# One Trainium2 kernel, one core: a list scheduler that knows the shared SBUF port, weight remainders on VectorE only, and float16 conversions on ScalarE or GpSimd

## The chip, the core and the metric

The kernel runs on one core of a Trainium2 chip. TensorE (PE in the profile; PEld is its weight load) multiplies, VectorE (DVE), ScalarE (ACT) and GpSimd (POOL) do the element-wise work, SyncE (SP) issues every DMA. The metric is device time in microseconds, the median of several executions. All times here are microseconds unless a row says ns.

## The reference, cut to what matters

```python
def _attn_ref(q, k, v, proj):                       # (2, 8, 768, 64), proj (64, 6)
    q_bucket = sum(((q @ proj) > 0) * powers)       # 6 hash bits
    k_bucket = sum(((k @ proj) > 0) * powers)
    scores = where(q_bucket == k_bucket, (q @ k.T) / 8, -1e9)
    attn = exp(scores - max(scores)); attn /= sum(attn) + 1e-9
    return attn @ v

def _moe_ref(x, domain_probs, w1, w2):              # x (1536, 512), 4 experts, F = 1024
    p = domain_probs / (domain_probs.sum(-1) + 1e-9)
    return sum(p[:, e:e+1] * (relu(x @ w1[e]) @ w2[e]) for e in range(4))

def _moe2_ref(x, w_in, w_out, g_ln):                # 512 -> 1024 -> 512
    h = x @ w_in
    solu = h * softmax(h)
    ln = (solu - mean(solu)) / sqrt(var(solu) + 1e-6) * g_ln
    return ln @ w_out
```

The three are chained: attention gives x, the experts take it, the second layer follows.

## The kernel before, in words

The 1536 tokens are four chunks of three tiles of 128. For each chunk come attention (8 heads), 32 expert steps, and the second layer. Precision is kept by splitting each factor into a high part and a remainder (the rounded value, and what rounding lost), so a product is three matmuls: high by high, high by remainder, remainder by high.

An expert step (`moe_a`, `moe_b`) is 12 matmuls of 384 columns (`PS<-xh,wsa` and `PS<-xl,wsa`) and 9 of 512 (`PS<-wsb,hh` and `PS<-wsb,hx`). Between them ScalarE writes the high part of the hidden values (`hh<-PS`) and VectorE their remainder (`hx<-PS,hh`). Weights come in two streams (`Stream`): a block of 128x1024 is loaded (`wra`, `wrb`), ScalarE rounds it (`wsa<-wra`, `wsb<-wrb`), and a subtraction makes the remainder (`wsa<-wra,wsa`, `wsb<-wrb,wsb`). That subtraction runs on GpSimd for all 64 first-layer expert blocks and for the 16 second-layer blocks of the first chunk, on VectorE for the rest.

Attention of the first chunk comes first and alone (`attn_first`). That of each later chunk is spread over the expert steps of the chunk before it (`attn_steps`, `Fill`). A row of 128 queries goes through scores (`PS<-kC,qC`, `PS<-kB,qB`), row maximum on VectorE (`sm<-PS`), two one-column instructions, the exponential on ScalarE (`p<-PS,sm`), a float16 high part on ScalarE (`h<-p,sm`) and its remainder on VectorE (`l<-p,sm,h`). The scores' PSUM buffer exists once (`s_b`, cap 1), so the next row's scores wait for this row's exponential. Two transposing DMAs bring a row's float16 parts into a buffer `t16`; after three rows, two conversions of 128x2304 elements to the type of the matmul (`t<-t`, line 886) follow, and `PS<-t,vs` multiplies with v. Conversions run on GpSimd (`pcopy`). The float64 weights of the second layer are decoded during the first chunk's experts (`decode_steps`: `ln<-ln`, later `y<-y`).

The order of all this is not written by hand. `Recorder` takes the instructions in program order, finds which needs which, and `emit` lays them out by a list schedule: it holds a clock and, for each engine, a heap of instructions that are ready; a free engine takes the one with the lowest place in program order (`turn_at`, less an advance given by `ahead`). How long an instruction takes in this plan is the estimate of `cost`; how long the next one must wait behind it is in `HOPS` and `OWN`. On the chip the engines then run their lists in that order, each waiting for what it needs.

Of the kernel before, what the change touches and what calls it, by code (L numbers as in the profile page):

```python
# [23 lines left out]
class Line:  # L24
    """PSUM buffers that get their places in program order."""
# [4 lines left out]
class Bank:  # L30
    """A kind of PSUM buffer: n banks in a row from one of `starts`, at most `cap` of it in use at once."""
# [10 lines left out]
class Slot:  # L42
    """A PSUM buffer whose place is chosen when the instructions are put in order."""
# [9 lines left out]
class View:  # L53
    """A part of a Slot, seen as an access pattern."""
# [28 lines left out]
class Recorder:  # L83
    """Takes the instructions in program order and emits them in an order in which the
    engines wait little: a list schedule over the dependences between the regions they touch."""

    READS = ("in_", "in0", "in1", "lhsT", "rhs", "identity", "scalar", "scalar1", "scalar2", "scale", "bias")
    # from the end of an instruction to the start of one that needs it, by their engines
    HOPS = dict(AG=0.17, AT=0.16, AV=0.1, GT=0.13, GV=0.1, TA=0.2, TG=0.22, TV=0.2, VA=0.2, VG=0.18, VT=0.2)
    OWN = dict(A=0.05, G=0.1, V=0.1, T=0.0)  # L90
# [10 lines left out]
    def engine(self, name):  # L101
        rec = self

        class Engine:
            def __getattr__(self, method):
                return lambda **kw: rec.add(name, method, kw)

        return Engine()

    @contextmanager  # L110
    def ahead(self, n):
        """Instructions that go before others of up to n places earlier."""
        self.boost += n
        yield
        self.boost -= n

    @contextmanager
    def group(self):
        """Instructions of one engine that stay together."""
        self.open = dict(eng=None, calls=[], cost=0.0, reads=[], writes=[], slots=[])  # L120
        yield
        op, self.open = self.open, None
        if op["calls"]:
            self.commit(op)
# [52 lines left out]
    def cost(self, name, method, kw, reads):  # L177
        out = kw["out"] if "out" in kw else None
        n = 1
        for d in list(out.ap)[1:]:  # L180
            n *= d[1]
        ptr = 0.06 * sum(1 for key in ("scalar", "scalar1", "scalar2") if not isinstance(kw.get(key, 0.0), (int, float, type(None))))
        if name == "T":
            if method == "transpose":
                return 0.057 if kw["in_"].dtype == F32R else 0.108
            return n * (4 if kw["rhs"].dtype == F32 else 1) / 2400 + 0.003
        if name == "A":
            ptr = 0.093 * sum(1 for key in ("scale", "bias") if not isinstance(kw.get(key, 0.0), (int, float)))
            psum = str(kw["in_"].space).endswith("PSUM")
            return (0.05 if psum else 0.092) + n / 1200 + ptr + (0.09 if "accum_out" in kw else 0)  # L190
        if name == "V":
            if method == "tensor_reduce":
                n = 1
                for d in list(kw["in_"].ap)[1:]:
                    n *= d[1]
                return 0.065 + n / 960
            fast = method in ("tensor_scalar", "tensor_copy") and not str((kw.get("in0") or kw.get("in_")).space).endswith("PSUM")
            return 0.065 + n / (1920 if fast else 960) + ptr
        if name == "G":
            return 0.095 + n * (2.16 if method == "tensor_tensor" else 0.9) / 1000  # L200
        size = SIZE[out.dtype]
        for d in list(out.ap)[:1]:
            n *= d[1]
        return n * size / 360e3

    def add(self, name, method, kw):
        def aps(keys):
# [4 lines left out]

        fn = getattr(self.engines[name], method)
        reads = [self.region(x) for x in aps(self.READS)]
        writes = [self.region(x) for x in aps(("out", "accum_out"))]
        cost = self.cost(name, method, kw, reads)
        if method == "memset":
            kw = dict(ap=kw["out"], constant=kw["value"])
        op = dict(
            eng=name,  # L220
            calls=[(fn, kw)],
            cost=cost,
            reads=reads,
            writes=writes,
            turn=method == "dma_start_transpose",
# [6 lines left out]
        assert g["eng"] in (None, name)  # L232
        g["eng"] = name
        g["turn"] = False
        g["calls"] += op["calls"]
        g["cost"] += op["cost"]
# [27 lines left out]
    def emit(self):  # L264
# [12 lines left out]
        wire = 0.0  # L277
# [14 lines left out]

        for i in range(n):
            if not left[i]:
                heappush(events, (0.0, i, None))
        order = []
        now = 0.0
        while len(order) < n:
            while events and events[0][0] <= now + 1e-9:
                _, i, slot = heappop(events)  # L300
                if slot is not None:
# [3 lines left out]
                    for j in blocked:  # L305
                        heappush(ready[ops[j]["eng"]], (ops[j]["turn_at"], j))
                    blocked.clear()
                elif i >= 0:
                    heappush(ready[ops[i]["eng"]], (ops[i]["turn_at"], i))
            for e in ready:  # L310
                if free[e] > now + 1e-9:
                    continue
                while ready[e]:
                    i = heappop(ready[e])[1]
                    if all(x.base is not None or place(x) for x in ops[i]["slots"]):
                        break
                    blocked.append(i)
                else:
                    continue
                if any(x.kind.line for x in ops[i]["slots"]):  # L320
                    for j in blocked:
                        heappush(ready[ops[j]["eng"]], (ops[j]["turn_at"], j))
                    blocked.clear()
                o = ops[i]
                order.append(i)
                if e == "S":
                    free[e] = now + (1.18 if o["turn"] else 0.48)
                    wire = max(wire, now + 1.2) + (0.67 if o["turn"] else o["cost"])
                    done = wire + 0.95
# [7 lines left out]
                for j in users[i]:  # L337
                    to = ops[j]["eng"]
                    hop = 0.0 if e == "S" else self.OWN[e] if to == e else self.HOPS.get(e + to, 0.1)
# [12 lines left out]
def lsh_attention_moe_solu(  # L352
# [28 lines left out]
    # rows of hash bits: 8 for a bit's product with its complement on the other side, 8 for the reverse  # L381
# [3 lines left out]
    # the order of the weight streams holds for these  # L385
# [11 lines left out]
    # token tiles: tile r of batch b holds the tokens 6 p + r  # L397
# [16 lines left out]
    class Ring:  # L414
        """Buffers that are used in turn."""
# [57 lines left out]

    def sub(eng, out, a, b):
        eng.tensor_tensor(out=out, in0=a, in1=b, op=ALU.subtract)

# [15 lines left out]
    def consts_a():  # L492
        """What the projections need: column h*128 + 8j + h, and 64 on its low part, of lhs_w is projection j for head h."""
# [22 lines left out]
    # rows of kD: low parts, high parts, bits; of qD: high, low, high, bits  # L516
# [6 lines left out]
    def proj_steps(c, is_k, nat, tb, pp, stks, br=None, hls=hl_r, heads=range(H)):  # L523
        """Split k or q into parts, transpose them, write stacks and hash bits."""
# [63 lines left out]
        # every product of rows is 0 for equal bits and -C for unequal ones, so a match adds exact zeros only  # L588
# [49 lines left out]
    def row_max(ps, E):  # L638
# [5 lines left out]
        # a row without a match has the same weight everywhere  # L644
# [58 lines left out]
    def row(U, rr, sb, E, pr_=p_r):  # L703
        """Probabilities of 128 queries, not yet divided by their sum."""
# [7 lines left out]
    def attn_first():  # L712
        """Projections and attention of the first chunk: nothing else runs yet."""
# [22 lines left out]
        # stacks of all heads stay where the first weights will go  # L736
# [24 lines left out]
        # the heads from FH on use float32 products: they cost the tensor engine more and the others less  # L761
# [25 lines left out]
        # two buffers for probabilities: tiles of keys 0-3 and 4-5, high and low parts  # L787
# [70 lines left out]
    def attn_steps(c):  # L858
# [8 lines left out]
        for h in range(H):  # L867
# [17 lines left out]
            for a in range(2):  # L885
                pcopy(t32[:, a, :, 0:N], d16[:, a, :, 0:N])
# [10 lines left out]
    def decode_steps(units, n, buf):  # L897
        """float64 to float32, n columns at a time: (source, factor per row or None, destination)."""
# [6 lines left out]
        for i, (src, g, dst) in enumerate(units):  # L905
# [4 lines left out]
            # exponent field to float32's, cut off at zero and infinity  # L910
# [3 lines left out]
            # mantissa in [1, 2], its 52 bits rounded to float32's  # L914
# [25 lines left out]
    def decode_a():  # L940
        """w_in and the first rows of w_out."""
# [12 lines left out]
    class Stream:  # L954
        """Weights in the order of use: [128, 4, 256] or [128, 2, 512], split into parts."""
# [10 lines left out]
        def load(self, i):  # L966
            while self.nl <= min(i, len(self.items) - 1):
                t = wr_r[self.kind].next()
                SP.dma_start(out=t, in_=self.items[self.nl][0])
# [3 lines left out]
        def split(self, i):  # L973
            while self.ns <= min(i, len(self.items) - 1):
# [4 lines left out]
                sub(self.items[self.ns][1], w[1], t, f(w[0]))  # L979
# [10 lines left out]
    def add_moe1(c, lo, hi):  # L990
        for m in range(lo, hi):
            e, fp = divmod(m, NF // 2)
            i1["m", c, m] = len(W1.items)
            W1.items.append((w1[e][:, fp * 256:fp * 256 + 256].rearrange("(k p) f -> p k f", p=128), G))
# [420 lines left out]
```

## Time and profile before

| | us |
|---|---|
| median of 3 timed runs | 1026.81 (1024.26 to 1030.49) |
| span of the profiled execution | 1014.7 |
| PE busy | 922.6 (91%) |
| DVE busy | 719.9 (71%) |
| ACT busy | 533.6 (53%) |
| POOL busy | 427.9 (42%) |

The page of the profiled execution gives as its own time the span from its first to its last instruction, 1014.7 us; the median of the timed runs is 12.1 us above it. Busy is time in which an engine executes, its waits for a port inside an instruction included.

### The profile page before, as it was taken

To read this page: it belongs to the slowest core of one execution; us is meant where nothing else is said; L and a number is where in the kernel's file an instruction comes from. 1 tells how busy PE (TensorE), PEld (TensorE's weight loads), DVE (VectorE), ACT (ScalarE), POOL (GpSimd) and SP (SyncE) were. 2 spreads that over 40 slices of the span, in tenths; PEclk is the share of its full clock that TensorE was granted. 3 is DMA by queue.
4 is the path that set the end of the run, shared out by engine and by line. 5 is a ranking of instruction groups with operands and counts; after the bars stand their busy time and mean duration, and the time that the engine had idled before them with its cause. 6 is when DMAs were issued, how large, how long until landed. Compare 5 with 4: busy or idle time off the path is not lost. (4 is left out here: it accounts for less than half of the span.)

```text
span 1014.7 us, 14292 instructions
## 1 busy us (share of the span) xinstructions
PE 922.6 (91%) x4864; PEld 818.1 (81%) x4864; DVE 719.9 (71%) x1242; ACT 533.6 (53%) x855; POOL 427.9 (42%) x333
## 2 busy tenths in 40 slices
PE   6789799787879998999999999999999999999997
PEld 5576688676768887887788898798889897999986
DVE  5765567999898888778877569868874556343564
ACT  4667346554544565665556457655553464333433
POOL 5568446575575152246444414344644031122100
PEclk9899899999998999999999999999999999999999
DMA  7166788998877786799879668868863333433400
GB/s 186 40 194 203 233 226 187 244 224 199 225 200 194 243 282 213 187 235 224 188 172 264 187 167 184 227 180 206 207 167 116 123 104 125 155 126 125 157 31 31
DMA packets 216809, 182.20 MB, mean 180 GB/s; under 512 B 127520, under 2 KB 183712, under 8 KB 216736
## 3 DMA queue, kind: packets, MB, share of 16 engines
q1 hardware_dynamic: 216736, 181.29, 66.5%
q8 instruction: 38, 0.62, 0.2%
q14 instruction: 35, 0.29, 0.1%
HBM read 127.89 MB, written 22.09 MB: 148 GB/s over the span
## 5 line engine op out<-in xcount | busy, mean ns | idle before, releaser
L348 PE MATMUL PS<-xh,wsa 128*128 128x384 f32 x1024 | 289.3, 344 | 16.2 <-DVE hx L348 8.1
L348 PE MATMUL PS<-wsb,hh 128*128 128x512 f32 x928 | 295.3, 400 | 0.5 <-DVE y L348 0.5
L348 POOL TENSOR_TENSOR wsa<-wra,wsa 128x1024 fp32r<-128x1024 f32 x64 | 160.1, 2502 | 286.9 <-ACT wsa L348 281.5
L348 PEld LDWEIGHTS PS<-xh,wsa 128*128 128x128 f32 x1024 | 192.1, 193 | 24.3 <-DVE hx L348 9.6
L348 PEld LDWEIGHTS PS<-wsb,hh 128*128 128x128 f32 x928 | 172.7, 191 | 25.9 <-DVE y L348 1.0
L348 PE MATMUL PS<-wsb,hx 128*128 128x512 f32 x464 | 185.0, 399 | 0.8 <-DVE hx L348 0.8
L348 PE MATMUL PS<-xl,wsa 128*128 128x384 f32 x512 | 174.8, 342 | 0.0
L348 POOL TENSOR_SCALAR t<-t 128x2304 fp32r<-128x2304 f16 x48 | 119.4, 2498 | 87.2 <-DMA t<-h 74.9
L348 ACT ACTIVATE p<-PS,sm 128x768 f32<-128x768 f32 x96 | 95.1, 991 | 103.2 <-DVE sm L348 86.3
L348 ACT ACTIVATE hh<-PS 128x384 fp32r<-128x384 f32 (+2 forms) x162 | 77.8, 485 | 119.5 <-PE PS L348 118.8
L348 DVE TENSOR_TENSOR wsb<-wrb,wsb 128x1024 fp32r<-128x1024 f32 x62 | 97.4, 1572 | 38.1 <-ACT wsb L348 37.7
L348 DVE SCALAR_TENSOR_TENSOR l<-p,sm,h 128x768 f16<-128x768 f32 x72 | 107.1, 1488 | 16.9 <-ACT h L348 16.7
L348 DVE SCALAR_TENSOR_TENSOR hx<-PS,hh 128x384 fp32r<-128x384 f32 x128 | 70.2, 549 | 63.9 <-ACT hh L348 63.2
L348 DVE TENSOR_REDUCE sm<-PS 128x1 f32<-128x768 f32 x96 | 91.0, 951 | 20.5 <-PE PS L348 19.8
L348 PEld LDWEIGHTS PS<-wsb,hx 128*128 128x128 f32 x464 | 88.5, 191 | 21.0 <-DVE hx L348 1.5
L348 ACT ACTIVATE wsb<-wrb 128x1024 fp32r<-128x1024 f32 x78 | 82.5, 1057 | 40.4 <-PE PS L348 30.3
L348 PEld LDWEIGHTS PS<-xl,wsa 128*128 128x128 f32 x512 | 98.9, 193 | 4.3
L348 ACT ACTIVATE wsa<-wra 128x1024 fp32r<-128x1024 f32 x78 | 82.1, 1053 | 14.5 <-PE PS L348 8.6
L348 ACT ACTIVATE h<-p,sm 128x768 f16<-128x768 f32 x72 | 67.2, 933 | 35.5 <-issue 21.9
L348 PE MATMUL PS<-kC,qC 128*128 128x384 f32 x144 | 52.4, 364 | 21.6 <-ACT p L348 21.3
L348 PE MATMUL PS<-kB,qB 80*128 80x384 f32 x192 | 67.1, 349 | 4.8 <-DMA qB<-qD 4.8
L348 PE MATMUL PS<-t,vs 128*128 128x384 f32 x312 | 61.7, 343 | 4.9 <-ACT stk L348 1.4
(169 smaller groups left out, 1330.5 us busy)
## 6 DMA issues: line engine op xcount, KB each, us to landing
wra<-in_moe_w_dram SPq DMA_DIRECT2D x64, 512.0 KB, 4.0
wrb<-in_moe_w_dram SPq DMA_DIRECT2D x64, 512.0 KB, 4.4
kC<-kD SPq DMA_DIRECT2D x24, 384.0 KB, 3.9
wra<-winD SPq DMA_DIRECT2D x16, 512.0 KB, 3.7
wrb<-woutD SPq DMA_DIRECT2D x16, 512.0 KB, 4.3
kB<-kD SPq DMA_DIRECT2D x24, 240.0 KB, 4.4
vr<-in_v_dram SPq DMA_DIRECT2D x28, 192.0 KB, 3.8
qD<-stk SPq DMA_DIRECT2D x27, 192.0 KB, 4.0
```

Source lines behind the costliest of these rows:

```text
L348: fn(**{key: x.at(x.slot.base) if isinstance(x, View) else x for key, x in kw.items()})
```

## The change: what it does

Four things are edited (the comments are also taken out).

1. The plan's estimates: each matmul costs 12.5 ns over its columns, where it was 3 ns; hops, DMA times and small instructions get new values.
2. The plan has a lock named `port`. GpSimd's instructions other than memsets, VectorE's with two SBUF inputs, and VectorE's copies and scalar operations from SBUF hold it; none of them is started in the plan while another holds it.
3. All remainders of weights are subtracted on VectorE.
4. An instruction may have forms on several engines. The two conversions of a head have one on ScalarE and one on GpSimd; the plan gives them to the engine that is free first. It has put 26 of the 48 on ScalarE, 22 on GpSimd.

```diff
-    HOPS = dict(AG=0.17, AT=0.16, AV=0.1, GT=0.13, GV=0.1, TA=0.2, TG=0.22, TV=0.2, VA=0.2, VG=0.18, VT=0.2)
-    OWN = dict(A=0.05, G=0.1, V=0.1, T=0.0)
+    HOPS = dict(AG=0.2, AT=0.17, AV=0.15, GA=0.2, GT=0.18, GV=0.13, TA=0.22, TG=0.22, TV=0.22, VA=0.13, VG=0.18, VT=0.18)
+    OWN = dict(A=0.05, G=0.22, V=0.11, T=0.0)
...
-            return n * (4 if kw["rhs"].dtype == F32 else 1) / 2400 + 0.003
+            return (n * 4 / 2400 + 0.004 if kw["rhs"].dtype == F32 else n / 2400 + 0.0125), False
...
+            two = n > 2 and sum(not psum(x) for x in ins) == 2
+            fast = n > 2 and method in ("tensor_scalar", "tensor_copy") and not psum(ins[0])
+            ptr = 0.06 * (tensor("scalar") + tensor("scalar1") + tensor("scalar2"))
+            return 0.066 + n / (1920 if fast else 960) + ptr + (0.07 if "accum_out" in kw else 0), two or fast
         if name == "G":
-            return 0.095 + n * (2.16 if method == "tensor_tensor" else 0.9) / 1000
+            if method == "tensor_tensor":
+                return 0.04 + n * 2.27 / 1000, True
+            return (0.19 if n <= 2 else 0.045 + n * 0.93 / 1000), method != "memset"
...
+                    if o["forms"][e]["port"] and port > now + 1e-9:
+                        later.append(i)
...
+                    if form["port"]:
+                        port = done
...
+    def copy_by(names, out, in_):
+
+        forms = dict(
+            G=("tensor_scalar", dict(out=out, in0=in_, scalar1=1.0, scalar2=1.0, op0=ALU.mult, op1=ALU.mult)),
+            A=("activation", dict(out=out, in_=in_, func=ACTF.Copy)),
+            V=("tensor_copy", dict(out=out, in_=in_)),
+        )
+        rec.add([(name, *forms[name]) for name in names])
...
-                pcopy(t32[:, a, :, 0:N], d16[:, a, :, 0:N])
+                copy_by("AG", t32[:, a, :, 0:N], d16[:, a, :, 0:N])
...
-                sub(self.items[self.ns][1], w[1], t, f(w[0]))
+                sub(V, w[1], t, f(w[0]))
```

The order moves on every engine. On POOL, in the first chunk's expert steps while the second chunk's attention runs beside them, this stood before (`ln` is the decoding, `t_86` the converted probabilities, `vs` the high part of v):

```order
L348 TENSOR_SCALAR ln_113<-ln_113 128x512
L348 TENSOR_TENSOR wsa_106<-wra_102,wsa_106 128x1024
L348 TENSOR_TENSOR wsb_109<-wrb_105,wsb_109 128x1024
L348 TENSOR_TENSOR wsa_107<-wra_103,wsa_107 128x1024
L348 TENSOR_TENSOR wsb_108<-wrb_104,wsb_108 128x1024
L348 TENSOR_SCALAR t_86<-t_84 128x2304 x2
L348 TENSOR_TENSOR wsa_106<-wra_102,wsa_106 128x1024
L348 TENSOR_TENSOR wsb_109<-wrb_105,wsb_109 128x1024
L348 TENSOR_SCALAR vs_74<-vr_73 128x6x64
L348 TENSOR_SCALAR ln_113<-ln_113 128x512
```

At the same place POOL now has:

```order
L387 TENSOR_SCALAR ln_113<-ln_113 128x512
L387 TENSOR_SCALAR t_86<-t_84 128x2304
L387 TENSOR_SCALAR vs_74<-vr_73 128x6x64
L387 TENSOR_SCALAR ln_113<-ln_113 128x512
L387 TENSOR_SCALAR t_86<-t_85 128x2304
L387 TENSOR_SCALAR ln_113<-ln_113 128x512
```

The subtractions have left, and of each pair of conversions one is left. On DVE, a little earlier in the same steps, the row maxima and the decoding stood like this before:

```order
L348 SCALAR_TENSOR_TENSOR hx<-PS,hh 128x384
L348 TENSOR_SCALAR ln_113<-ln_113 128x512 x3
L348 SCALAR_TENSOR_TENSOR ln_113<-ln_113 128x512 x2
L348 TENSOR_TENSOR ln_113<-ln_113 128x512
L348 SCALAR_TENSOR_TENSOR hx<-PS,hh 128x384
L348 TENSOR_REDUCE sm_87<-PS 128x1
L348 TENSOR_SCALAR sm_87<-sm_87 128x1 x3
```

Now the subtractions of both weight streams stand between them:

```order
L387 TENSOR_TENSOR wsa_107<-wra_103,wsa_107 128x1024
L387 TENSOR_TENSOR wsb_108<-wrb_104,wsb_108 128x1024
L387 SCALAR_TENSOR_TENSOR hx<-PS,hh 128x384
L387 TENSOR_SCALAR ln_113<-ln_113 128x512 x3
L387 SCALAR_TENSOR_TENSOR ln_113<-ln_113 128x512 x2
L387 SCALAR_TENSOR_TENSOR hx<-PS,hh 128x384
L387 TENSOR_TENSOR ln_113<-ln_113 128x512
L387 TENSOR_TENSOR wsa_106<-wra_102,wsa_106 128x1024
L387 TENSOR_TENSOR wsb_109<-wrb_105,wsb_109 128x1024
L387 SCALAR_TENSOR_TENSOR hx<-PS,hh 128x384
L387 TENSOR_REDUCE sm_87<-PS 128x1
```

So VectorE has two more instructions of 1024 elements in front of a row maximum. On ACT, in the same steps, a conversion now stands between a row's high part and the next row's exponential:

```order
L387 ACTIVATE hh<-PS 128x384
L387 ACTIVATE p_79,sm_88<-PS,sm_88 128x768
L387 ACTIVATE h_81<-p_79,sm_88 128x768
L387 ACTIVATE t_86<-t_84 128x2304
L387 ACTIVATE p_77,sm_89<-PS,sm_89 128x768
L387 ACTIVATE ln_113<-ln_113 128x512
L387 ACTIVATE hh<-PS 128x384
```

Before, no instruction on ACT was of this size: the conversion was POOL's.

## Rows read from the trace of the kernel before

**Rows 1.** The page: span, and busy time of each engine.

```profile
span 1014.7 us, 14292 instructions
...
PE 922.6 (91%) x4864; PEld 818.1 (81%) x4864; DVE 719.9 (71%) x1242; ACT 533.6 (53%) x855; POOL 427.9 (42%) x333
```

**Rows 2.** Windows: busy time by engine in six stages; PEclk is the granted clock.

```profile
0.00:108.00 108.00, 86.92 (x452) 70.12 (x452) 67.68 (x134) 65.40 (x130) 65.42 (x139) 0.94 0.56 163
108.00:340.00 232.00, 195.45 (x951) 172.41 (x950) 194.91 (x292) 116.01 (x182) 134.02 (x74) 0.95 0.83 212
340.00:424.00 84.00, 75.85 (x445) 67.82 (x445) 73.01 (x154) 50.74 (x88) 28.47 (x27) 0.96 0.77 237
424.00:662.00 238.00, 224.56 (x1197) 201.17 (x1196) 185.05 (x330) 140.27 (x221) 103.78 (x54) 0.99 0.85 205
662.00:968.00 306.00, 299.88 (x1572) 271.31 (x1571) 172.24 (x259) 144.92 (x211) 96.23 (x41) 1.00 0.51 148
968.00:1014.70 46.70, 39.90 (x258) 35.25 (x256) 27.00 (x79) 16.29 (x26) 0.00 (x0) 1.00 0.08 29
```

**Rows 3.** Windows: a stretch of the last chunk's expert steps, same columns.

```profile
862.00:962.00 100.00, 100.00 (x504) 90.52 (x503) 42.50 (x49) 38.57 (x52) 23.95 (x10) 1.00 0.41 136
```

**Rows 4.** Waits of PE from 108 to 340 us: in total, times, longest.

```profile
PE PS L348 <- ACT p L348: 12.4, 11, 3.0
```

**Rows 5.** Groups by form, DVE, 108 to 340 us: busy, mean ns.

```profile
L348 DVE SCALAR_TENSOR_TENSOR l<-p,sm,h 128x768 f16<-128x768 f32 x24 | 37.9, 1579 | 5.6 <-ACT h L348 5.6
L348 DVE TENSOR_SCALAR ln<-ln 128x512 int32<-128x512 int32 x36 | 32.9, 950 | 3.3 <-DMA ln<-in_moe_w_in_dram 3.2
...
L348 DVE SCALAR_TENSOR_TENSOR ln<-ln 128x512 int32<-128x512 int32 x12 | 12.6, 1049 | 0.6 <-POOL ln L348 0.5
L348 DVE SCALAR_TENSOR_TENSOR ln<-ln 128x512 f32<-128x512 uint32 x12 | 12.5, 1038 | 0.4 <-ACT ln L348 0.4
...
L348 DVE TENSOR_TENSOR ln<-ln 128x512 f32<-128x512 f32 x8 | 11.3, 1410 | 0.1
L348 DVE TENSOR_TENSOR hl<-vr,hl 128x384 fp32r<-128x384 f32 x7 | 9.4, 1342 | 0.0
L348 DVE TENSOR_TENSOR vs<-vr,vs 128x384 fp32r<-128x384 f32 x8 | 8.6, 1070 | 0.3 <-POOL vs L348 0.3
```

**Rows 6.** Timeline of DVE, five stretches: start, duration of single or merged instructions.

```profile
139.11 0.69 DVE L348 TENSOR_TENSOR ln<-ln 128x512 f32<-128x512 f32 x1
...
243.12 0.55 DVE L348 TENSOR_TENSOR vs<-vr,vs 128x384 fp32r<-128x384 f32 x1
...
245.21 1.08 DVE L348 TENSOR_SCALAR ln<-ln 128x512 int32<-128x512 int32 x3
...
398.88 1.22 DVE L348 TENSOR_TENSOR wsb<-wrb,wsb 128x1024 fp32r<-128x1024 f32 x1
...
405.12 1.01 DVE L348 SCALAR_TENSOR_TENSOR l<-p,sm,h 128x768 f16<-128x768 f32 x1
```

**Rows 7.** Timeline of DVE and POOL around 249 us.

```profile
248.60 2.90 DVE L348 SCALAR_TENSOR_TENSOR ln<-ln 128x512 int32<-128x512 int32 x1
...
248.55 2.41 POOL L348 TENSOR_TENSOR wsa<-wra,wsa 128x1024 fp32r<-128x1024 f32 x1 [1.55 <-ACT wsa L348]
```

**Rows 8.** Groups by form, POOL, 108 to 340 us.

```profile
L348 POOL TENSOR_TENSOR wsb<-wrb,wsb 128x1024 fp32r<-128x1024 f32 x15 | 39.9, 2661 | 6.0 <-ACT wsb L348 6.0
L348 POOL TENSOR_SCALAR t<-t 128x2304 fp32r<-128x2304 f16 x16 | 37.4, 2348 | 12.3 <-DMA t<-h 6.9 <-DMA t<-l 5.2
L348 POOL TENSOR_TENSOR wsa<-wra,wsa 128x1024 fp32r<-128x1024 f32 x15 | 37.4, 2491 | 45.2 <-ACT wsa L348 43.8 <-DMA kB<-kD 1.4
```

**Rows 9.** Groups by form, whole span: POOL's moved work, ACT's nearest copy.

```profile
L348 POOL TENSOR_TENSOR wsa<-wra,wsa 128x1024 fp32r<-128x1024 f32 x64 | 160.1, 2502 | 286.9 <-ACT wsa L348 281.5 <-PE PS L348 3.9 <-DMA kB<-kD 1.4
L348 POOL TENSOR_SCALAR t<-t 128x2304 fp32r<-128x2304 f16 x48 | 119.4, 2498 | 87.2 <-DMA t<-h 74.9 <-DMA t<-l 7.1 <-issue 3.7
...
L348 ACT ACTIVATE wsb<-wrb 128x1024 fp32r<-128x1024 f32 x78 | 82.5, 1057 | 40.4 <-PE PS L348 30.3 <-issue 4.4 <-DMA wrb<-woutD 2.7
```

More of the change, by code (lines that the diff above doesn't have):

```diff
@@ L118, in group @@
     def group(self):
-        self.open = dict(eng=None, calls=[], cost=0.0, reads=[], writes=[], slots=[])
+        self.open = dict(forms={}, turn=False, reads=[], writes=[], slots=[])
         yield
         op, self.open = self.open, None
-        if op["calls"]:
+        if op["forms"]:
             self.commit(op)
@@ L175, in covers, with cost, size @@
         return x[0] <= y[0] and y[1] <= x[1] and all(any(a <= c and d <= b for a, b in x[2]) for c, d in y[2])
[L177 to L182, printed above, removed]
+    @staticmethod
+    def cost(name, method, kw):
+        tensor = lambda key: kw.get(key) is not None and not isinstance(kw[key], (int, float))
+        psum = lambda ap: str(ap.space).endswith("PSUM")
+        def size(ap):
+            n = 1
+            for d in list(ap.ap)[1:]:
+                n *= d[1]
+            return n
+        n = size(kw["out"])
@@ L197, in cost @@
-            fast = method in ("tensor_scalar", "tensor_copy") and not str((kw.get("in0") or kw.get("in_")).space).endswith("PSUM")
-            return 0.065 + n / (1920 if fast else 960) + ptr
-        if name == "G":
-            return 0.095 + n * (2.16 if method == "tensor_tensor" else 0.9) / 1000
-        size = SIZE[out.dtype]
+                return 0.063 + size(kw["in_"]) / 960, False
+            if method in ("reciprocal", "memset"):
+                return 0.07 + n / 960, False
+            ins = [kw[key] for key in ("in_", "in0", "in1") if tensor(key)]
@@ L202, in cost, with add, aps @@
+        out = kw["out"]
+        parts = 128
+        for ap in (out, kw["in_"]):
+            if str(ap.space).endswith("SBUF"):
+                parts = list(ap.ap)[0][1]
         for d in list(out.ap)[:1]:
             n *= d[1]
-        return n * size / 360e3
-    def add(self, name, method, kw):
-        def aps(keys):
+        return n * SIZE[out.dtype] / 360e3 * (1.0 if parts > 96 else 1.6), False
+    def add(self, forms):
+        def aps(kw, keys):
             for key in keys:
@@ L231, in add @@
         g = self.open
[L232 to L236, printed above, removed]
+        (name, form), = made.items()
+        if g["forms"]:
+            old = g["forms"][name]
+            old["calls"] += form["calls"]
+            old["cost"] += form["cost"]
+        else:
+            g["forms"] = {name: dict(form, cost=form["cost"] + 0.012)}
         g["slots"] += [x for x in op["slots"] if x not in g["slots"]]
@@ L276, in emit @@
         blocked = []
-        wire = 0.0
+        wire = port = 0.0
         events = []
@@ L291, in place, with offer, unblock @@
             return False
+        def offer(i):
+            for e in ops[i]["forms"]:
+                heappush(ready[e], (ops[i]["turn_at"], i))
+        def unblock():
+            for j in blocked:
+                offer(j)
+            blocked.clear()
         for i in range(n):
@@ L304, in emit @@
                     k.live -= 1
[L305 to L307 removed]
+                    unblock()
                 elif i >= 0:
[L309 removed]
+                    offer(i)
             for e in ready:
```

82 lines of the change are left out of this document (44 added, 38 removed).

## The prediction

> **What bounds the kernel now.** First the page: TensorE is busy for 922.6 of 1014.7 us, so 92.1 us is all that it stands idle [rows 1]. Then the windows, to see where: 21.1 us of that lie before 108 us (the first chunk's attention), 36.6 between 108 and 340 (the first chunk's experts, the second chunk's attention and the decoding), 8.2 up to 424, 13.4 up to 662, 6.1 up to 968 and 6.8 in the tail [rows 2]. The reader should see that the second stage is the odd one. There VectorE is busy for 194.9 of 232 us, 84%, as busy as TensorE with 195.5; from 662 us on it has 56% and TensorE 98%.
>
> How much TensorE must do there comes from the last chunk's steps, where it never stops: 504 matmuls, 24 steps of 21, in 100.0 us, 0.198 us each [rows 3]. The 951 matmuls of the stage, some of them short transposes, need at most 951 x 0.198 = 188 us. So up to 44 of its 232 us are to be had by TensorE, idle time and lower clock together: the granted clock there is 0.95 in the mean, which between the levels of 1.2 and 2.4 GHz means a tenth of the stage at the lower one [rows 2]. I give the clock no term of its own, since TensorE isn't what the stage waits for.
>
> What VectorE does in those 194.9 us is read from the groups by form [rows 5] against single instructions of the same forms elsewhere [rows 6]. The remainder `l` takes 1.579 us in the mean and 1.01 alone; a decoding scalar instruction 0.950, and 0.36 when three in a row take 1.08; the two-input decoding forms 1.049, 1.038 and 1.410 against 0.69; `hl` 1.342 and `vs` 1.070 against 0.55, the time of `vs` alone for the same 384 elements. The excess is 24 x 0.57 + 36 x 0.59 + 12 x 0.36 + 12 x 0.35 + 8 x 0.72 + 7 x 0.79 + 8 x 0.52 = 59 us: 30% of VectorE's busy time in the stage is waiting inside instructions. For whom, a pair of rows shows: GpSimd's subtraction runs from 248.55 to 250.96, and VectorE's 0.69 us instruction, started at 248.60, ends at 251.50 [rows 7].
>
> The Trainium skill (SBUF — State Buffer, section "SBUF: two separate sides") says why: VectorE with two SBUF inputs or in a two-port mode and GpSimd share one port pair, and whoever comes first keeps it to the end of its instruction. These two rows agree.
>
> **Subtractions, 80 of them, from GpSimd to VectorE.** They leave GpSimd at 2.5 us each [rows 8, 9]. On VectorE one costs 1.22 us alone [rows 6]. Between 108 and 340 us there are 30, which is 36.6 us more work for VectorE.
>
> **Conversions, 26 of 48 to ScalarE, nine of them in this stage.** They leave GpSimd at 2.35 us there [rows 8]. No row has this copy on ScalarE. Its 1024-element copy takes 1.057 us [rows 9]; 2304 elements can't take less, and not more than 2.25 times as long, 2.38 us, as the part that doesn't grow is multiplied too. I take 2.3, near the upper end, because most of it should grow. ScalarE then has 116 + 9 x 2.3 = 137 us of work in the stage, under two thirds of it, so the forecast gives this nothing.
>
> **Waits that go.** GpSimd's 134.0 us in the stage lose 39.9 + 37.4 for subtractions and 9 x 2.35 = 21.1 for conversions; 35.6 us are left, 27% [rows 2, 8]. I let VectorE's waits shrink alike: 59 to 16, so 43 go. The bounds are 59 (all gone) and nothing. VectorE's sum is 194.9 + 36.6 - 43 = 188.5 us, hardly less than before. That is the main point: moving the work costs nearly what the port gives back.
>
> **What the stage gains.** What remains is how densely VectorE can work. With 84%, as now, the stage takes 188.5 / 0.84 = 224.4 us (-7.6). In the next stage, where GpSimd is busy for only a third of the time, VectorE reaches 73.0 of 84 us, 87% [rows 2]. After the change GpSimd is quieter than that in both, and fewer stalls of 2 us fall into the chain from scores over row maximum to exponential, for which TensorE waits 12.4 us [rows 4]. I take 87%: 216.7 us, **-15.3**. At 92% it would be 204.9 (-27.1), still above TensorE's 188.
>
> **The other stages.** From 340 to 424 VectorE is at 87% already; five subtractions come (6.1 us), and the waits for them go: **0**, between -3 and +6. From 424 to 662 TensorE is at 94%, VectorE at 78%, and 13.4 us of idle can go; there the plan's better picture helps, and I take half, **-6.7**. From 662 to 968 half of 6.1 us, **-3**: only small gains are left under a TensorE at 98%. Before 108 us two or three subtractions leave the end of GpSimd's queue: **-3** of 21.1 idle, which otherwise belong to a chain of dependences. The tail has no GpSimd work [rows 2]: **0**.
>
> **The new estimates.** The old plan thought an expert step took 12 x 0.163 + 9 x 0.216 = 3.90 us, the new one 12 x 0.1725 + 9 x 0.2258 = 4.10; the chip takes 100.0 / 24 = 4.17 [rows 3]. Under the old plan VectorE and ScalarE lag behind a TensorE that in the plan is 6% too fast. Its price is contained in the halves above. DMA estimates change order alone, not the number of issues; I give them nothing, within 3 us either way.
>
> **The sum.** -15.3 + 0 - 6.7 - 3 - 3 + 0 = -28. From a span of 1014.7 to 986.7. The median of the runs lies 12.1 us above the profiled span, which I carry: 1026.8 - 28 = 999 us.
>
> **Rivals.**
>
> *Slower: VectorE becomes the bound of the second stage.* If the waits don't shrink, its sum is 194.9 + 36.6 = 231.5 us; even at 92% that takes 251.6, +19.6, and the halves of the later stages are lost with it; -3 of the head stays: 1026.8 + 16.6 = 1043 us. For it: two subtractions now stand in front of a row maximum, and the queue is in order. Against it: 73% of GpSimd's time in the stage goes. It decides where less than 36.6 of the 59 us of waiting go.
>
> *Every remaining GpSimd instruction blocks one of VectorE's for its whole length.* Then 35.6 us of waiting stay, 23.4 go, the sum is 208.1, at 87% 239.2 us: +7.2, in all 1026.8 + 7.2 - 12.7 = 1021 us. Against it: before, 134.0 us of GpSimd cost VectorE 59, 44% and not all. The rule of the Trainium skill cited above (SBUF — State Buffer, the exclusive port pair), taken at its strictest, gives this case.
>
> *ScalarE holds up TensorE.* A conversion in front of an exponential or of `hh` delays it by up to 2.3 us. If a third of the 26 do so in full, 20 us are lost: 1019 us; with 12 of 26 the gain of 28 is gone. For it: the order puts one right in front of an exponential. Against it: ScalarE is idle for 47% of the span [rows 1], and TensorE has other steps ready.
>
> *Nothing.* The stage keeps its 84%, and the new order brings as many stalls as it takes away: about 1027 us.
>
> *More than forecast.* The second stage at 92%, all 13.4 and 6.1 us of idle gone, twice the gain in the head: -27.1 - 13.4 - 6.1 - 6 = -52.6, 974 us.
>
> **How the numbers follow.** Forecast (985 to 1012) 0.52, more 0.10, the whole-length blocking 0.09, ScalarE 0.07, nothing 0.08, slower 0.14. For this kernel a difference of 0.5%, 5.1 us, is about what a measurement can tell: faster means under 1021.7, slower over 1031.9. The forecast, the larger gain and some 0.10 of the next two cases are faster: 0.72. The rest of those two and the nothing are the same: 0.14. Slower: 0.14. The range goes from the larger gain, 974, to the end of no change, 1031; the slower case stays outside. The likeliest case alone has 985 to 1012.
>
> **What would show it.** VectorE's total busy time should stay about the same, 720 plus 98 for 80 subtractions less about as much waiting; above 760, the waits stayed. GpSimd's should fall to 428 - 160 - 42 - 65, about 160 us, ScalarE's rise by 60 to about 594. `l` should fall from 1.58 us to about 1.2 in the second stage; above 1.4 speaks for one of the first two rivals. The second stage, from the first `PS<-xh,wsa` to the transposes of `y`, should take about 217 us; 230 or more with VectorE over 90% is the slower case. A ScalarE rival shows as TensorE waiting for `hh` or `p` behind `t<-t`. The prediction is wrong at its root if the waits vanish and the second stage still doesn't shorten: then the chain of dependences, not VectorE's load, sets its length.

## The result, and the profile after

The changed kernel takes 977.01 us (median of 4, 973.27 to 984.94) against 1025.74 (median of 4): a ratio of 0.9554, 95% interval 0.9524 to 0.9584. It is 4.5% faster. The time is 22 us below the 999 that were forecast, inside the range of 974 to 1031 and near its lower end, but outside the 985 to 1012 of the case that was called the likeliest.

The page of the changed kernel, span and busy time, answers to [rows 1]:

```profile
span 983.2 us, 14195 instructions
...
PE 920.0 (94%) x4864; PEld 820.0 (83%) x4864; DVE 694.3 (71%) x1322; ACT 582.5 (59%) x881; POOL 152.0 (15%) x227
```

VectorE has 80 instructions more and is busy for 25.6 us less. GpSimd came down to 152.0 us, near the 160 foreseen; ScalarE came out 12 us under the 594.

The windows of the changed kernel, cut at the same places of the program as [rows 2] (first `PS<-xh,wsa`, first `PS<-idn,y`, end of the first group of `PS<-idn,ln`, end of the second, start of the last layer); columns as there:

```profile
0.00:116.40 116.40, 93.28 (x451) 75.78 (x452) 69.98 (x139) 64.95 (x131) 57.91 (x135) 0.87 0.51 154
116.40:312.00 195.60, 185.27 (x955) 166.83 (x954) 169.64 (x322) 133.34 (x192) 37.97 (x38) 0.98 0.96 252
312.00:389.00 77.00, 71.57 (x435) 63.57 (x434) 68.01 (x158) 49.44 (x85) 10.94 (x20) 1.00 0.84 254
389.00:628.00 239.00, 226.16 (x1209) 203.87 (x1207) 179.49 (x348) 164.20 (x233) 31.75 (x28) 0.99 0.85 205
628.00:933.40 305.40, 301.40 (x1572) 272.97 (x1571) 180.67 (x283) 155.47 (x216) 13.47 (x7) 0.99 0.52 147
933.40:983.20 49.80, 42.31 (x253) 36.97 (x251) 26.48 (x77) 15.15 (x25) 0.00 (x0) 0.93 0.08 27
```

The second stage went from 232 us to 195.6. That is the whole result: the other five stages sum to +4.9 (+8.4, -7.0, +1.0, -0.6, +3.1). The cuts of [rows 2] are rounded and lie up to 2.5 us beside these places of the program; at the places themselves the six stages of before have 108.7, 231.2, 82.4, 237.3, 309.5 and 45.7 us, and the changes are +7.8, -35.5, -5.1, +2.0, -4.7 and +4.0. The head and the tail are longer in this execution, at a granted clock of 0.87 and 0.93; the end of this document comes back to that.

Of the 36.4 us of the second stage, 26.2 are idle time of TensorE, which went from 36.6 to 10.3 us; the other 10.2 are its busy time, 195.5 to 185.3, beside a granted clock that rose from 0.95 to 0.98. What TensorE no longer waits for is above all VectorE's remainder `hx`, in the stage before:

```profile
PE PS L348 <- DVE hx L348: 10.6, 3, 5.4
```

and all its waits in the stage of the changed kernel:

```profile
PE PS L387 <- ACT p L387: 9.0, 8, 2.7
PE PS L387 <- DVE wsb L387: 0.6, 1, 0.6
PE PS L387 <- ACT stk L387: 0.3, 1, 0.3
PE PS L387 <- DVE sm L387: 0.2, 1, 0.2
```

The wait for the exponential, the one that the prediction named [rows 4], went only from 12.4 to 9.0 us. The longest wait for `hx` before shows how the port reached TensorE:

```profile
298.08 4.86 DVE L348 TENSOR_SCALAR ln<-ln 128x512 int32<-128x512 int32 x2
...
303.11 2.33 DVE L348 SCALAR_TENSOR_TENSOR ln<-ln 128x512 f32<-128x512 uint32 x1
305.36 0.54 DVE L348 SCALAR_TENSOR_TENSOR hx<-PS,hh 128x384 fp32r<-128x384 f32 x1
```

```profile
297.82 2.58 POOL L348 TENSOR_TENSOR wsb<-wrb,wsb 128x1024 fp32r<-128x1024 f32 x1
300.38 4.53 POOL L348 TENSOR_SCALAR t<-t 128x2304 fp32r<-128x2304 f16 x2
```

```profile
305.96 0.69 PE L348 MATMUL PS<-xh,wsa 128*128 128x384 f32 x1 [5.45 <-DVE hx L348]
```

While GpSimd has a subtraction and then two conversions, VectorE's decoding takes 4.86 us for two instructions of 0.36 alone, and 2.33 for one of 0.69 [rows 6]. `hx` stands behind them in VectorE's order, and TensorE is idle for 5.45 us until it is written.

The groups by form of VectorE in the second stage of the changed kernel answer to [rows 5]:

```profile
L387 DVE SCALAR_TENSOR_TENSOR l<-p,sm,h 128x768 f16<-128x768 f32 x24 | 26.3, 1098 | 5.5 <-ACT h L387 5.5
...
L387 DVE TENSOR_TENSOR wsb<-wrb,wsb 128x1024 fp32r<-128x1024 f32 x16 | 21.4, 1335 | 0.9 <-ACT wsb L387 0.9
L387 DVE TENSOR_TENSOR wsa<-wra,wsa 128x1024 fp32r<-128x1024 f32 x17 | 20.6, 1215 | 0.8 <-ACT wsa L387 0.8
...
L387 DVE TENSOR_SCALAR ln<-ln 128x512 int32<-128x512 int32 x34 | 13.2, 425 | 0.0
...
L387 DVE SCALAR_TENSOR_TENSOR ln<-ln 128x512 f32<-128x512 uint32 x12 | 8.7, 726 | 0.7 <-ACT ln L387 0.7
L387 DVE SCALAR_TENSOR_TENSOR ln<-ln 128x512 int32<-128x512 int32 x12 | 8.5, 711 | 0.1
...
L387 DVE TENSOR_TENSOR ln<-ln 128x512 f32<-128x512 f32 x8 | 5.6, 705 | 0.1
...
L387 DVE TENSOR_TENSOR vs<-vr,vs 128x384 fp32r<-128x384 f32 x8 | 4.4, 545 | 1.2 <-POOL vs L387 1.2
L387 DVE TENSOR_TENSOR hl<-vr,hl 128x384 fp32r<-128x384 f32 x7 | 3.8, 547 | 1.0 <-POOL hl L387 1.0
```

Every form that the prediction counted is now near the time that it takes alone [rows 6]: `l` 1.098 us against 1.01, `vs` and `hl` 0.55, the decoding 0.71 to 0.73 against 0.69. Of the 59 us of waiting that the prediction counted, about 5 are left (24 x 0.09 + 34 x 0.07 + 12 x 0.04 + 12 x 0.02 + 8 x 0.02). The moved subtractions wait a little as well: `wsb` takes 1.335 us against 1.22, 1.8 us over the 16.

The conversions on both engines, whole span of the changed kernel:

```profile
L387 POOL TENSOR_SCALAR t<-t 128x2304 fp32r<-128x2304 f16 x22 | 50.6, 2301 | 283.3 <-DMA t<-l 80.5
...
L387 ACT ACTIVATE t<-t 128x2304 fp32r<-128x2304 f16 x26 | 55.4, 2132 | 27.9 <-DMA t<-l 12.2
```

One on ScalarE takes 2.13 us, inside the bounds 1.06 and 2.38 and below the 2.3 taken.

### The profile page after: what moved, and what is told of

The parts are those of the page before. It is cut to its first block, busy times and chain, and to the rows that moved or that the text cites. A ratio compares the mean times of both kernels' runs of the same rounds, so it can differ in the third digit from the quotient of the medians.

```text
span 983.2 us, 14195 instructions
## 1 busy us (share of the span) xinstructions
PE 920.0 (94%) x4864; PEld 820.0 (83%) x4864; DVE 694.3 (71%) x1322; ACT 582.5 (59%) x881; POOL 152.0 (15%) x227
## 5 line engine op out<-in xcount | busy, mean ns | idle before, releaser
L387 PE MATMUL PS<-xh,wsa 128*128 128x384 f32 x1024 | 282.9, 337 | 0.0
L387 PEld LDWEIGHTS PS<-xh,wsa 128*128 128x128 f32 x1024 | 187.4, 188 | 5.4 <-DVE hx L387 0.5
L387 PE MATMUL PS<-xl,wsa 128*128 128x384 f32 x512 | 171.9, 336 | 0.0
L387 DVE TENSOR_TENSOR wsa<-wra,wsa 128x1024 fp32r<-128x1024 f32 x78 | 95.7, 1228 | 16.6 <-ACT wsa L387 16.0
L387 PEld LDWEIGHTS PS<-xl,wsa 128*128 128x128 f32 x512 | 96.2, 188 | 4.5
L387 POOL TENSOR_SCALAR t<-t 128x2304 fp32r<-128x2304 f16 x22 | 50.6, 2301 | 283.3 <-DMA t<-l 80.5
L387 DVE SCALAR_TENSOR_TENSOR l<-p,sm,h 128x768 f16<-128x768 f32 x72 | 77.7, 1080 | 15.3 <-ACT h L387 15.2
L387 ACT ACTIVATE t<-t 128x2304 fp32r<-128x2304 f16 x26 | 55.4, 2132 | 27.9 <-DMA t<-l 12.2
L387 PE MATMUL PS<-kB,qB 80*128 80x384 f32 x192 | 69.8, 364 | 1.0 <-DMA qB<-qC 0.9
```

The lines of the kernel that those rows point to most:

```text
L387: fn(**{key: x.at(x.slot.base) if isinstance(x, View) else x for key, x in kw.items()})
```

## The experiments

Each run gives its second stage as one line of the windows (columns as in [rows 2]), cut at the same two places. The changed kernel has 195.6 us there, the kernel before 231 between exactly these places. A line is of one execution, and any edit of the plan also changes the order of all engines; the scan of matmul lengths below shows how much another order alone can do.

**Only the subtractions move; the plan is that of before.**

```diff
-                sub(self.items[self.ns][1], w[1], t, f(w[0]))
+                sub(V, w[1], t, f(w[0]))
```

> The kernel before, its plan unchanged, with one edit: all 80 remainders of weights move from GpSimd to VectorE (conversions stay on GpSimd). Load theory (the gain comes from GpSimd's instructions leaving the port): most of the gain of the whole change, 990 to 1000 us, and the remainder l of the probabilities, 1.579 us in the second stage of before, falls to about 1.25. Plan theory (the gain comes from a plan that keeps port instructions apart): less than a third of the gain, 1012 us or more, l still above 1.35.

1002.47 us, ratio 0.976 (0.9716 to 0.9804). The windows of this run:

```profile
108.40:328.40 220.00, 194.07 (x951) 172.81 (x950) 188.56 (x323) 115.97 (x183) 60.98 (x46) 0.94 0.85 227
```

Between the two theories in time: 22 of the 49 us. `l` has 1.268 us in the stage, near the 1.25 of the load theory, so more than half of what it waited before went with the moved work under the old plan. The stage is 11 us shorter, and VectorE's sum, 188.6 us, is hardly lower than before: here the moved work does cost nearly what the waits give back, as the prediction had it for the whole change.

**Only the plan changes: new estimates and lock, but subtractions and conversions where they were.**

```diff
-                sub(V, w[1], t, f(w[0]))
+                sub(self.items[self.ns][1], w[1], t, f(w[0]))
...
-                copy_by("AG", t32[:, a, :, 0:N], d16[:, a, :, 0:N])
+                copy_by("G", t32[:, a, :, 0:N], d16[:, a, :, 0:N])
```

> The changed kernel with its new estimates and its lock, but subtractions and conversions on the engines of before (64 + 16 subtractions and all 48 conversions on GpSimd). Load theory: the port is wanted as much as before, so 1010 to 1030 us, and l stays near 1.5 us. Plan theory: 995 us or less, l under 1.25 us, because the same instructions no longer meet.

1025.96 us, ratio 0.9994 (0.9961 to 1.0028): no change. The edit also puts the engine of each subtraction back into the lists of weight blocks. The windows, and VectorE's `l` over the whole span of this run:

```profile
115.30:346.40 231.10, 199.44 (x954) 178.29 (x952) 185.11 (x291) 116.04 (x184) 137.41 (x75) 0.92 0.80 210
```

```profile
L387 DVE SCALAR_TENSOR_TENSOR l<-p,sm,h 128x768 f16<-128x768 f32 x72 | 102.5, 1423 | 14.2 <-ACT h L387 10.6 <-DMA t<-l 3.4
```

In the second stage alone `l` has 1.578 us, the 1.579 of before. A plan that knows of the port doesn't help while GpSimd is busy for 137 of 231 us. The theory that the plan brings the gain by itself has fallen.

**The changed kernel without the lock in the plan.**

```diff
-                    if o["forms"][e]["port"] and port > now + 1e-9:
+                    if False:
```

> The changed kernel, but the plan starts port instructions without regard to each other (estimates, moved subtractions and chosen conversions stay). Load theory: within 8 us of the changed kernel (970 to 985), VectorE's waits little higher, l 1.15 us. Plan theory: 990 us or more, with l in the second stage at 1.25 us or above, the 27% of waits that the prediction left.

993.09 us, ratio 0.9683 (0.9636 to 0.9729): 16 us slower than the changed kernel.

```profile
114.50:318.40 203.90, 188.47 (x951) 168.79 (x948) 177.61 (x321) 129.99 (x189) 42.01 (x37) 0.97 0.93 243
```

The stage is 8 us longer, VectorE's sum 8 us higher. `l` has 1.114 us in the stage against 1.098, far from the 1.25 of the plan theory: its forecast of the time came true, its reason did not. The load theory, 970 to 985 us, missed the time.

**The changed kernel with the old length of a matmul in the plan.**

```diff
-            return (n * 4 / 2400 + 0.004 if kw["rhs"].dtype == F32 else n / 2400 + 0.0125), False
+            return (n * 4 / 2400 + 0.004 if kw["rhs"].dtype == F32 else n / 2400 + 0.003), False
```

> The changed kernel, but the plan thinks again that a matmul costs 3 ns over its columns, where it was 12.5. Load theory: within 5 us of the changed kernel. A third theory, that the longer matmuls in the plan bring the gain in the stages where TensorE is the bound: 10 us or more slower than the changed kernel, the loss between 312 and 763 us of the trace, as idle time of TensorE before scores and before the second product.

964.08 us, ratio 0.938 (0.9334 to 0.9425): faster than both kernels, which no theory had expected. The second stage is 2 us longer than the changed kernel's:

```profile
112.50:310.30 197.80, 188.00 (x951) 169.24 (x950) 170.01 (x321) 131.76 (x192) 37.87 (x37) 0.97 0.92 248
```

**The changed kernel with the subtractions back on GpSimd.** The edit is the first pair of lines of the plan-only run.

> The changed kernel, but the 80 subtractions go back to GpSimd (estimates, lock and chosen conversions stay). If the moved subtractions carry the gain: 1005 us or more, the second stage at 215 us or more and l there above 1.3 us, though the plan has the lock. If the chosen conversions carry as much: 995 us or less. With so much GpSimd work left the plan should give more than 30 of the 48 conversions to ScalarE.

990.14 us, ratio 0.9653 (0.9613 to 0.9692), 13 us slower than the changed kernel. The plan gave 30 conversions to ScalarE, one fewer than expected at the least. The windows, and the two groups that tell the most, over the whole span:

```profile
114.10:314.10 200.00, 185.34 (x954) 167.69 (x953) 159.35 (x292) 140.85 (x197) 104.56 (x64) 0.98 0.95 244
```

```profile
L387 DVE SCALAR_TENSOR_TENSOR l<-p,sm,h 128x768 f16<-128x768 f32 x72 | 82.7, 1150 | 9.6 <-ACT h L387 9.6
...
L387 ACT ACTIVATE t<-t 128x2304 fp32r<-128x2304 f16 x30 | 63.8, 2128 | 25.9 <-DMA t<-h 19.7 <-DMA t<-l 3.9 <-issue 2.1
```

The moved subtractions don't carry the gain alone: without them the stage is 200.0 us. Against the plan-only run the one edit is that conversions may go to ScalarE, and by the two ratios some 35 us are gained. VectorE's sum fell from 185.1 to 159.4 us, 26 us, though no work was taken from it: GpSimd had 33 us less. So the conversions hold VectorE up too, and by these sums more per us than the whole of GpSimd's work did before (26 of 33 against 59 of 134). VectorE is at 80% of the stage, and the stage is no shorter than the changed kernel's: from about 200 us on VectorE isn't its bound. TensorE, with 185 of 200, is nearer to it.

**The changed kernel with all conversions on GpSimd.** The edit is the second pair of lines of the plan-only run.

> The changed kernel, but all 48 conversions stay on GpSimd (estimates, lock and moved subtractions stay). By the port: 26 more holders of 2.3 us, 60 us, of which VectorE paid before 44% as waiting, 26 us over the span, less what the lock in the plan keeps apart; I expect 985 to 995 us. If the conversions don't matter: within 5 us of the changed kernel. If ScalarE held TensorE up by them: faster than the changed kernel.

983.37 us, ratio 0.9584 (0.9536 to 0.9633): 6 us over the changed kernel, less than expected, and the intervals of the two overlap. So a gain from the conversions on top of the moved subtractions isn't shown.

```profile
109.40:320.00 210.60, 192.39 (x957) 172.17 (x956) 183.83 (x324) 117.29 (x185) 64.74 (x47) 0.95 0.90 237
```

The second stage itself is 15 us longer than the changed kernel's, with VectorE busy for 87% of it; the profiled span, 982.2 us, isn't. The head of this execution is 7 us shorter, which the end of this document takes up, and the fourth stage, cut as above, has 229.4 us against 239.3.

**Old estimates throughout, lock and moves kept.** Every duration and hop of the plan as before (`HOPS`, `OWN`, matmuls, DMA times, small instructions), as

```diff
-    OWN = dict(A=0.05, G=0.22, V=0.11, T=0.0)
+    OWN = dict(A=0.05, G=0.1, V=0.1, T=0.0)
...
-                    done = wire + 1.3
+                    done = wire + 0.95
```

> The changed kernel, lock, moved subtractions and chosen conversions kept, but with every duration and hop in the plan as before. The plan with 3 ns per matmul alone ran at 964 us, 13 under the changed kernel. If the other new estimates help: slower than 964, 968 to 980 us. If none of them helps: 964 or less, and the head, 108.7 us before and 112 to 117 in every run with the new estimates, is at 109 again.

981.18 us, ratio 0.9567 (0.952 to 0.9615).

```profile
114.30:315.80 201.50, 185.58 (x934) 168.98 (x933) 166.94 (x319) 131.95 (x187) 37.72 (x34) 0.96 0.91 240
```

Against the changed kernel's 0.9554 (0.9524 to 0.9584) the intervals overlap: as a set, the new estimates are worth nothing that shows. Neither forecast came true as a whole: the time is over both, and the head, at 114.3 us, did not go back to 109.

**The same without the lock: only the two moves.**

> Old durations and hops in the plan and no lock; only the subtractions on VectorE and the conversions on ScalarE or GpSimd. With the moved subtractions alone it was 1002 us. If the two moves together make nearly the whole gain: 980 us or less. If the lock is worth here what it is worth beside the new estimates (16 us): about 16 us over the run with old estimates and lock, 980 to 990 us.

990.89 us, ratio 0.9662 (0.9625 to 0.97).

```profile
107.80:315.90 208.10, 189.30 (x936) 170.15 (x935) 170.77 (x321) 129.44 (x187) 40.28 (x35) 0.94 0.89 234
```

The two moves under the old plan make 34 of the 49 us, not nearly the whole gain. The lock adds 10 here and 16 beside the new estimates, twice with the same sign; `l` in the stage hardly tells the runs with it (1.009 and 1.098 us) from those without (1.036 and 1.114). The scan below shows that another order alone makes as much, so its worth isn't settled.

**Three more lengths of a matmul in the plan: 0, 7.5 and 20 ns over the columns.**

```diff
-            return (n * 4 / 2400 + 0.004 if kw["rhs"].dtype == F32 else n / 2400 + 0.0125), False
+            return (n * 4 / 2400 + 0.004 if kw["rhs"].dtype == F32 else n / 2400 + 0.0), False
```

> The changed kernel, with 0 ns instead of 12.5 ns over the columns of a matmul in the plan. With 3 ns it ran at 964 us, with 12.5 at 977. Theory of a lead: a TensorE that is too fast in the plan puts its suppliers early in the order, so less is better: 964 us or a little less. Theory of scatter: any change of the estimates gives another order, and times fall between 960 and 990 us without regard to the direction.

> The changed kernel, with 7.5 ns instead of 12.5 over the columns. Theory of a lead: between the two, 968 to 973 us. Theory of scatter: anywhere between 960 and 990 us, outside 964 to 977 as likely as in it.

> The changed kernel, with 20 ns instead of 12.5 over the columns, more than the chip takes. Theory of a lead: slower than the changed kernel, 982 us or more, the loss as idle time of TensorE between 312 and 763 us. Theory of scatter: between 960 and 990 us, faster than 977 as likely as slower.

With the two known ones, in order of the estimate:

| ns over the columns | 0 | 3 | 7.5 | 12.5 | 20 |
|---|---|---|---|---|---|
| median, us | 981.93 | 964.08 | 985.96 | 977.01 | 999.72 |
| ratio to before | 0.9594 | 0.938 | 0.9642 | 0.9554 | 0.9766 |

The windows of the runs with 0, 7.5 and 20:

```profile
107.70:315.10 207.40, 190.28 (x951) 171.31 (x949) 171.63 (x321) 131.78 (x190) 41.36 (x36) 0.94 0.92 238
```

```profile
116.30:324.70 208.40, 189.56 (x940) 169.69 (x939) 168.84 (x320) 135.23 (x190) 34.88 (x33) 0.94 0.90 234
```

```profile
110.30:314.70 204.40, 186.63 (x939) 167.51 (x938) 173.99 (x320) 133.50 (x189) 38.04 (x34) 0.97 0.91 238
```

From 0 to 12.5 there is no direction, only 22 us between the best and the worst. The theory of a lead has fallen for these four; 20 ns, with which the plan's expert step has 12 x 0.18 + 9 x 0.233 = 4.26 us and so more than the chip's 4.17 [rows 3], is the slowest, but one point doesn't tell a trend from scatter.

**The changed kernel with all conversions on ScalarE.**

```diff
-                copy_by("AG", t32[:, a, :, 0:N], d16[:, a, :, 0:N])
+                copy_by("A", t32[:, a, :, 0:N], d16[:, a, :, 0:N])
```

> The changed kernel, but all 48 conversions on ScalarE (2.13 us each in the trace of the changed kernel; 22 more are 47 us of work for ScalarE). The rival of the prediction, that ScalarE holds TensorE up: 15 us or more slower than the changed kernel, 992 us or more, with TensorE waiting for hh or p. If the port is what counts: 22 holders of 2.3 us less, GpSimd near 100 us of busy time, VectorE's waits a few us less, and 970 to 980 us.

1003.47 us, ratio 0.9824 (0.9772 to 0.9877): 26 us slower than the changed kernel, though VectorE's `l` is down to 1.034 us and GpSimd to 99.0 us of busy time. The windows, and what TensorE waits for over the span, total, times, longest:

```profile
111.00:318.90 207.90, 189.79 (x939) 169.82 (x938) 166.56 (x320) 144.35 (x195) 18.46 (x28) 0.94 0.88 234
```

```profile
PE PS L387 <- ACT stk L387: 15.8, 9, 3.4
PE PS L387 <- ACT p L387: 15.7, 19, 2.4
```

In the changed kernel the same two waits are 4.9 and 18.8 us: the one for `stk` (transposed parts of q or k, which ScalarE copies out of PSUM) is 11 us longer, the one for `p` is not. The two longest waits of the stage that are put down to `stk`, 3.4 and 2.9 us, end with the two `stk` of these rows:

```profile
291.33 2.13 ACT L387 ACTIVATE t<-t 128x2304 fp32r<-128x2304 f16 x1
293.37 0.50 ACT L387 ACTIVATE xh<-xp 128x384 fp32r<-128x384 f32 x1
293.78 2.11 ACT L387 ACTIVATE t<-t 128x2304 fp32r<-128x2304 f16 x1
295.79 0.47 ACT L387 ACTIVATE stk<-PS 128x384 fp32r<-128x384 f32 x1
...
300.95 4.13 ACT L387 ACTIVATE t<-t 128x2304 fp32r<-128x2304 f16 x2
305.10 0.49 ACT L387 ACTIVATE stk<-PS 128x384 fp32r<-128x384 f32 x1
```

Each time `stk` stands behind two conversions, and so it does at a third wait of 3.4 us later in the span. So ScalarE does hold TensorE up, as the rival said, but not at `hh` and `p`, which it had named. The two profiled executions differ by 15.6 us in span, 12.3 of them in the second stage; the rest of the 26 us between the medians can't be placed, since the other executions have no trace.

## Why the prediction was right, and where its sizes were off

**Where the time lies: right.** The second stage was the one to shorten, by 36.4 us, more than the 31.5 us between the spans; the others together lost a little.

**What VectorE does there: right.** Time inside its instructions was waiting for GpSimd, and it went when GpSimd's work went: with the same work on VectorE, its sum in the stage is 185.1 us beside 137 us of GpSimd (plan alone) and 159.4 beside 105 (conversions on ScalarE too).

**Waits that go: mis-sized, and this is the step that failed.** The prediction shrank the waits in proportion to GpSimd's time, 59 to 16 us. Measured, 5 are left. In all, VectorE's sum of 194.9 took on about 38 us of subtractions (42.0 less the 3.9 of the two that it had already) and came out at 169.6, 63 us less than the two make together, where the prediction took off 43. By the groups, 54 us are the counted waits and 4 those of `ln<-ln,g_col`, which the prediction did not count (four instructions, 1.788 us before and 0.742 after); the last 5 aren't waiting that the rows show, as records of a queue overlap and the cuts of the stage differ a little. Whether the plan's lock did the rest, the runs don't settle. Without the lock the stage has 177.6 us of VectorE and not 169.6, which points to it; but with old estimates and no lock it has 170.8. In both VectorE's sum fell well below the 188.5 us of the proportional rule. So that rule was the mistake, and the run with the subtractions back shows the same: with 78% of GpSimd's time still in the stage, VectorE's sum is 35 us under that of before, where the rule would take off 13. Why so little is left to wait for isn't shown; what GpSimd keeps are short instructions and half of the conversions.

**What the stage gains: the density came out right, by luck.** 169.6 of 195.6 us is 87%, the value taken. With the measured sum in place of 188.5, the step gives 169.6 / 0.87 = 194.9 us. But five runs with nearly that sum, 167 to 172 us, have stages of 198 to 208 us, 81 to 86% (old estimates with and without the lock, and 0, 3 and 7.5 ns per matmul). And in the run with the subtractions back on GpSimd VectorE's 159 us left the stage at 200. A sum of VectorE doesn't give the length of the stage. The prediction's bound of 188 us for TensorE was near (185 busy), so below some 200 us the stage belongs to TensorE and to what stalls it. The path was only in part the one named: TensorE's wait for the exponential fell by 3.4 us, that for `hx` by 10.6. And the clock, given no term, has a share: the four runs with stages of 207 to 208 us have a granted clock of 0.94 there and TensorE busy for 189 to 190 us, the changed kernel 0.98 and 185.3.

**Subtractions and conversions: the order of the two was wrong.** The conversions were priced as a small relief beside the subtractions. Beside the new plan each move alone makes most of the gain: neither 1025.96 us, subtractions alone 983.37, conversions alone 990.14, both 977.01. The two don't add. In the second stage the conversions alone make even more: 231.1, 210.6, 200.0 and 195.6 us in the same order. With the conversions alone VectorE has 80% of the stage and isn't the bound, so that taking more waits from it can gain little; with the subtractions alone it has 87%, and why the whole kernel is no slower there isn't shown.

**The next stages.** Between the same places of the program, the stage from 340 us, given 0, gained 5.1, outside its bounds of -3 and +6. The next, given -6.7, lost 2.0: its idle time of 12.8 us stayed. The one after, given -3, gained 4.7. The scan of matmul lengths shows why no such terms could be given: an estimate moves the order, and the order moves the time by some 10 us either way.

**The head: wrong.** -3 was given. The +8.4 of this profile goes with a lower clock (last section); the same order took 109.4 us in another run, against 108.7 before, so no gain shows.

**The sum.** The 12.1 us carried from span to median were not what lies around a span. In the profiled execution of the changed kernel that is 1.7 us (984.94 against 983.2). If as much lies around that of before, its execution took 1016.4 us, less than any timed run of before in this study (the lowest has 1018.36), while the profile of after is of the slowest of its four. So the spans differ by 31.5 us and the medians by 48.7. That the spans come near the -28 of the sum is luck: the second stage gave 20 us more than its term, and the others made +4 to +5 where they were given -12.7. By the medians the forecast is 21 us short. No trace shows where the other executions differ from the profiled ones.

**The rivals.** VectorE as the bound wanted more than 22 us of waiting left (59 less 36.6), full blocking by what GpSimd keeps 35.6; there were about 5. Full blocking overrates the price: 38 us of GpSimd in the stage cost VectorE about 5. The Trainium skill (SBUF — State Buffer, section "SBUF: two separate sides") describes an exclusive port; that is not contradicted, and the pair in [rows 7] agrees with it. ScalarE holding up TensorE is real at 48 conversions (+26 us); at 26 no such loss shows. "Nothing" holds for the plan alone. "More than forecast", given 0.10, has the nearest time, 974 us, but not the cause: it wanted VectorE at 92% of the stage and all idle time of two later stages gone, and the stage has 87% of a smaller sum.

**A version that beats both** is the changed kernel with 3 ns per matmul in its plan, 964.08 us. The scan gives no sign that it is faster because of the estimate itself: 0 and 7.5 ns are both slower.

## What to carry to other kernels

Compare an instruction's mean in a busy stage with its time alone before you move work between engines: the difference is what the move can free, and here it paid for all of the moved work. Follow the waiting on to the engine that bounds the stage: what the late engine delays there need not be the chain that you looked at, as `hx` here. If two engines share a port, taking either large user off may make most of the gain, so test the parts singly before adding up their gains. With a list scheduler, a change of an estimate is also a draw of another order: 22 us between the best and the worst of four here, so try several and keep the best by measurement, and don't put such a difference down to the estimate. By that measure the 13 us of the subtractions on top of the conversions and the 10 and 16 of the lock are not settled; the 34 us and more of the moves are beyond it.

## What the runs showed of the hardware that was not expected

The head of the changed kernel and that of the run with all conversions on GpSimd have the same instructions in the same order on every engine, up to their first conversion, which is later. The first took 116.4 us to `PS<-xh,wsa`, the second 109.4. The windows of the same 40 us of the changed kernel and of that run:

```profile
20.00:60.00 40.00, 32.36 (x139) 28.86 (x140) 23.26 (x49) 19.87 (x43) 18.28 (x43) 0.66 0.18 47
```

```profile
20.00:60.00 40.00, 30.57 (x165) 26.77 (x166) 27.54 (x56) 24.58 (x53) 23.29 (x55) 0.85 0.20 52
```

The granted clock was 0.66 of full speed in the one and 0.85 in the other, means over its levels of 1.2 and 2.4 GHz, and the slower one got 26 matmuls fewer done. Whether the clock fell first or the stops came first the rows don't show. So one execution of the same order can differ from another by 7 us in a stage in which TensorE often stops, and a single profile can't tell a gain of that size there.
